# A fused attention and mixture-of-experts kernel: a newly searched order of the attention, a later place for the first weight loads, and nested conditional blocks at the end

## Chip, cores and metric

The kernel runs on one core of one Trainium2 chip. The metric is the device time of one execution in microseconds (us), from the first to the last instruction of the program with what lies around it. Before the change three executions took 914.98, 911.16 and 907.74 us; the median is 911.16 us.

## What is computed

Two layers follow one another. The first is causal attention with a decay, for 8 batches of 8 heads, 576 tokens and 64 numbers a head. The second sends each of the 4608 tokens to one of 8 experts, a two-layer network of its own.

```python
# attention, q k v: (8, 8, 576, 64), f: (8, 8, 576)
scores = q @ k.transpose(0, 1, 3, 2) / sqrt(64)
cum = cumsum(log(clip(f, 0.0001, 1.0)), axis=-1)
scores = where(causal, -1e9, scores + cum[..., :, None] - cum[..., None, :])
attn = exp(scores - max(scores)); attn = attn / (sum(attn) + 1e-9)
x = (attn @ v), heads side by side: (4608, 512)
# experts, w1: (8, 512, 1024), w2: (8, 1024, 512)
logits = x @ w_gate + modality_bias[modality_id]
e_idx = argmax(logits); gate_w = softmax(logits)[e_idx]
out[mask_e] = gate_w * (relu(x[mask_e] @ w1[e]) @ w2[e])
```

Products are split into high and low parts, so that each product of two tensors is three matmuls: high by high, high by low, low by high.

## The kernel before

**Attention, 32 pairs of heads.** Class `Attn` handles two heads (a pair, `p`) at a time. The work of a pair is cut into named steps, each a call of a small function on one engine: `hi` and `lo` split the loaded q and k (lines 347 and 353); `mm` (L486 to L497) are score matmuls for the row maxima, `mr` (L507 to L512) the maxima on VectorE; `sp` (L518) transposes them on TensorE, `ssp` (L524, L525) splits them, and `so` (L532, `shift_out`) stores them with two small DMAs into the tile `Sq`; `s` (L551 to L566) are the score matmuls that use `Sq`; `e` is the exponential, `h` and `r` split its result into `Ph` and `Pl` (L596, L604), `w` (L624 to L626) are the matmuls with v, and `d` (L635 to L640) divides by the row sum. Steps per batch prepare v (`v`, `vm`, `v1`, `v3`, `v2`, `vh`, `vl`), the gate (`vt`, `kg` at L437, `kh`, `kl`), and route and scatter the tokens (`ga`, `rt`, `sc`).

Matmuls of `mm` and `s` use 64 rows of TensorE's array, two heads beside one another; those of `w`, `kg`, `sp`, `rt` use 128 or fewer rows as one block. The profile writes the first as 64*128 and the second as 128*128.

**Who sets the order.** `Plan.order()` is a list scheduler. It holds every step's engine, a duration, its predecessors and the buffers it takes, and emits the steps one after another: among the ready ones the one whose earliest start is first, and where that is equal the one with the smaller due time, from the table `DUE`. The order it gives is the order of the program on each engine, since the attention runs under a manual schedule. The step `early`, put in when batch 5 has been scattered, makes the first table of the experts' tiles (25 small VectorE instructions, L915 to L986) and loads the first two tiles of tokens.

**Experts.** Class `Moe` takes the tokens, sorted by expert, in tiles of 256 (`FULL` = 21 of them at most) and then half tiles of 128 (8 at most). A tile `t` transposes its tokens (`prepare`), multiplies by w1 (`first`, L1083, 96 matmuls), by w2 (`second`, L1094, 48 matmuls) and scatters its rows with an indirect DMA on GpSimd (L1097). Meanwhile it loads the next weights on SyncE's queue (`load_w1` L1037, `load_w2` L1043) and splits them on ScalarE and VectorE (`split_w1` L1049 and L1050, `split_w2` L1056 and L1057). The loads of the first w1 (2 MB in two DMAs) are issued as soon as their space is free, in the place that the tile scheduler finds, which is inside the attention's last pairs.

How many tiles there are is known only on the chip. Tiles 0 to 13 always run. Tiles 14 to 20, and the 8 half tiles, each stand in a conditional block of their own, one after another; in this data 18 tiles and 3 half tiles run, so 3 blocks and then 5 blocks are skipped:

```python
            if t < ALWAYS:
                body()
            else:
                with self.tc.If(nt > t - EARLY):   # L1176
                    body()
        for t in range(8):
            with self.tc.If(nh > t):               # L1179
                self.half(t)
```

A skipped block still has to raise the semaphores that its instructions would have raised. On each engine that is a COMPARE_BRANCH and an EVENT_SEMAPHORE, and on GpSimd, for the DMAs that it would have issued, an INC_SWDGE_SEM. L1262 is the end of the program.

Of the kernel before, what the change touches and what calls it, by code (L numbers as in the profile page):

```python
# [26 lines left out]
P = 128  # L27
# [33 lines left out]
def f32(ap):  # L61
# [21 lines left out]
}  # L83


class Plan:


    LAT = {"PE": 0.15, "ACT": 0.15, "DVE": 0.1, "POOL": 0.18, "SP": 0.0}

    def __init__(self, rings):
        self.bufs = dict(rings)
        self.steps = {}

# [6 lines left out]
    def order(self):  # L101
# [8 lines left out]
        done, ef, dma = {}, dict.fromkeys(self.LAT, 0.0), 0.0  # L110
# [4 lines left out]
        while ready:  # L115
            best = None
            for n in ready:
                s = st[n]
                t = max((done[a] for a in s["after"]), default=0.0)
                blocked = False  # L120
                for j, (r, _) in enumerate(s["take"]):
                    k = len(taken[r]) - self.bufs[r] + j
                    if k >= 0:
                        x = given.get((r, taken[r][k]))
                        blocked = blocked or x is None
                        t = max(t, x or 0.0)
# [14 lines left out]
            for e, d in s["ops"]:  # L141
                port, e = e[3:] == "*", e.rstrip("*")
# [5 lines left out]
            if s["lands"] is not None:  # L148
                dma = max(dma, t) + s["lands"] / 190e3
# [21 lines left out]
class Attn:  # L171
# [355 lines left out]
    def shift_out(self, p):  # L527
# [3 lines left out]
        for a in range(2):  # L531
            self.nc.sync.dma_start(self.Sq[32 * a:P:64, p % 3, :], mT[:, a])  # L532
# [202 lines left out]
    def steps(self, early):  # L735
# [4 lines left out]
        def add(name, key, eng, t, fn, args, after=(), due=0.0, **kw):  # L740
# [8 lines left out]
            plan.add((name,) + key, ops, lambda: fn(*args), after, PER * at + DUE[kind], **kw)  # L749
# [4 lines left out]
        for p in range(n):  # L754
# [6 lines left out]
            add("hi", k, "ACT", 1.25, self.split_hi, k, [("raw", p) if p > 1 else None] + [prev("s", 3, g) for g in range(4)], d - 3)  # L761
            add("lo", k, "POOL" if p else "DVE", 2.8, self.split_lo, k, [("hi", p)], d + 2)
            add("cum", k, "SP", 0.55, self.put_cum, k, [prev("s", 3, g) for g in range(4)], d - 4, lands=10e3)
            for g in range(3):
                add("mm", k + (g,), "PE", (0.68, 0.68, 0.65)[g], self.max_mms, (p, g), [("hi", p), ("cum", p)], d + g,
                    take=[("ps", ("m", p, i)) for i in ((0,), (1,), (2, 3))[g]])
            for g in range(4):
                add("mr", k + (g,), "DVE", (1.4, 1.4, 0.77, 0.77)[g], self.max_red, (p, g),
                    [("mm", p, min(g, 2)), ("mr", p, 2) if g == 3 else None, prev("sp", 2)], d + g + 1, free=[("ps", ("m", p, g))])
            add("sp", k, "PE", 0.2, self.shift_pe, k, [("mr", p, g) for g in range(4)], d + 6, take=("pb", ("t", p)))  # L770
            add("ssp", k, "DVE", 0.6, self.shift_split, k, [("sp", p), prev("so", 2)], d + 6.3, free=[("pb", ("t", p))])
            add("so", k, "SP", 1.1, self.shift_out, k, [("ssp", p)] + [prev("s", 3, g) for g in range(4)], d + 7, lands=10e3)
            for g in range(4):
                add("s", k + (g,), "PE", (0.65, 0.55, 1.22, 1.17)[g], self.scores, (p, g), [("so", p), ("lo", p), ("cum", p)], d + 11 + g,
                    take=("ps", (p, g)))
                add("e", k + (g,), [("ACT", (0.74, 0.74, 1.08, 1.12)[g])], 0, self.exp, (p, g),
                    [("s", p, g)] + ([("e", p, 0)] if g == 1 else []), d + 12 + g,
                    free=[] if g == 2 else [("ps", (p, g))], take=None if g in (1, 2) else ("Pt", (p, max(g - 1, 0))))
            for i in range(3):
                gs = ((0, 1), (2,), (3,))[i]  # L780
                add("h", k + (i,), "ACT", (1.17, 1.02, 1.05)[i], self.half, (p, i),
                    [("e", p, g) for g in gs] + ([("w", 2 * p - 4), ("w", 2 * p - 3)] if p > 1 else [("setup2",)]), d + 13.5 + i)
                add("r", k + (i,), "DVE" if i == 1 else "POOL", (2.4, 1.21, 2.33)[i], self.rest, (p, i), [("h", p, i)], d + 15 + i,
                    free=[("ps", (p, 2)) if i == 1 else ("Pt", (p, i))])
            for h in range(2):
                u = 2 * p + h
                add("w", (u,), "PE", 1.55, self.weighted, (u,), [("r", p, i) for i in range(3)] + [("vl", b, c) for c in range(NJ)] + [("kl", b, p % 4)],
                    d + 19 + h, take=("po", u))
                add("d", (u,), "DVE", 1.12, self.divide, (u,),
                    [("w", u), ("gb", b)] + ([("sc", b - 2, c) for c in range(NJ)] if b > 1 else []), d + 20.5 + h, free=[("po", u)])  # L790
        for b in range(nb):
# [7 lines left out]
            for i in range(3):  # L799
                add("vm", k + (i,), "DVE", (1.2, 1.2, 0.7)[i], self.v_max, (b, i),  # L800
# [7 lines left out]
            for i in range(3):  # L808
                add("vh", k + (i,), "ACT", (1.15, 1.15, 0.72)[i], self.v_hi, (b, i),
                    [("v2", b), ("setup2",)] + ([("w", NH * (b - 1) - 1)] if b > 1 else []), d - 9 + i)  # L810
            for c in range(NJ):
                add("vl", k + (c,), "DVE*", 0.75, self.v_lo, (b, c), [("vh", b, c // 2)] + ([("w", NH * (b - 1) - 1)] if b > 1 else []), d - 7 + c)
            add("gb", k, "ACT", 0.3, self.gate_bias, k, [("gs",), ("setup2",), bp("ga", 2)], d - 5)
            add("gv", k, "ACT", 0.25, self.gate_part, k, [("gs",), ("v2", b), bp("kg", 2, 3)], d - 11)
            for hp in range(4):
# [4 lines left out]
                add("kg", k + (hp,), "PE", 1.22, self.key_gate, (b, hp), [("vt", b, hp), ("gv", b), ("kg",) + divmod(4 * b + hp - 1, 4) if b or hp else None] + free, d - 6 + hp, take=("pb", ("kg", b, hp)))  # L820
                add("kh", k + (hp,), "ACT", 0.3, self.key_gate_hi, (b, hp), [("kg", b, hp), ("setup2",)], d - 5.5 + hp)
                add("kl", k + (hp,), "DVE", 0.3, self.key_gate_lo, (b, hp), [("kh", b, hp)], d - 5 + hp, free=[("pb", ("kg", b, hp))])
# [10 lines left out]
            for c in range(NJ):  # L833

                add("sc", k + (c,), "POOL", 1.25, self.scatter, (b, c), [("sc", b, c - 1) if c and b < nb - 1 else ("rt", b, 6)], e + 8 + c, lands=263e3)
# [30 lines left out]
class Moe:  # L866
    def __init__(self, keep, tc, w1, w2, xs, writers, out):
# [18 lines left out]
        self.xgh, self.xhh, self.xlh = {}, {}, {}  # L886

    def open(self, ctx):
        ec, tc = ctx.enter_context, self.tc
        w = "tile"  # L890
        px = [ec(tc.tile_pool(name="c_px", bufs=1, space=PSUM, reuse_waits=w))]
        self.ps_h = ec(tc.tile_pool(name="c_ph", bufs=3, space=PSUM, reuse_waits=w))
        self.ps_y = ec(tc.tile_pool(name="c_py", bufs=2, space=PSUM, reuse_waits=w))
        px.append(ec(tc.tile_pool(name="c_px1", bufs=1, space=PSUM, reuse_waits=w)))
        self.px = lambda i: px[i].tile([P, 512], F32, name=f"px{i}")
# [8 lines left out]
        self.hx = ec(tc.tile_pool(name="c_hx", bufs=3, reuse_waits=w))  # L904
# [119 lines left out]
    def load_x(self, t):  # L1024
        nc = self.nc
        r = self.val(self.row[t], 1, 8 * (CAP // T) - 1)
        xg = self.keep.tile([P, 2, 514], F32, name="xg", bufs=3)
# [4 lines left out]
    def load_w1(self, row, i=0):  # L1032
# [3 lines left out]
        for q in range(2):  # L1036
            nc.sync.dma_start(self.raw1[i][:, :, q * 512:q * 512 + 512], w1[:, :, q * 512:q * 512 + 512], cond=self.ec[1])  # L1037
# [21 lines left out]
    def prepare(self, t):  # L1059
# [3 lines left out]
        xh = self.xp.tile([P, 4, T], F32R, name="xh", bufs=2)  # L1063
        xl = self.xp.tile([P, 4, T], F32R, name="xl", bufs=2)
# [23 lines left out]
    def second(self, xg, n):  # L1088
        nc = self.nc
        for c in range(n):  # L1090
            py = self.ps_y.tile([P, 512], F32, name="py")
# [3 lines left out]
            y = self.wk.tile([P, 512], F32, name="y", bufs=2)  # L1095
# [5 lines left out]
    def load_xh(self, t):  # L1101
        nc = self.nc
        r = self.val(self.rowh[t], 1, 8 * (CAP // T) - 1)
        xg = self.hx.tile([P, 514], F32, name="hxg", bufs=3)
# [3 lines left out]
    def prepare_h(self, t):  # L1108
        nc = self.nc
        xh = self.wk.tile([P, 4, P], F32R, name="hxh", bufs=2)  # L1110
        xl = self.wk.tile([P, 4, P], F32R, name="hxl", bufs=2)
# [7 lines left out]
    def first_h(self, t):  # L1119
# [3 lines left out]
        hb = self.wk.tile([P, 2, 512], F32, name="hb", bufs=1)  # L1123
        for q in range(2):
            ph = self.ps_h.tile([P, 2, T], F32, name="ph").rearrange("p a n -> p (a n)")
# [18 lines left out]
    def run(self, acc):  # L1144
        self.load_w1(self.row[0])
# [3 lines left out]
        self.prepare(0)  # L1149
        for t in range(FULL):  # L1150
# [22 lines left out]
            if t < ALWAYS:  # L1173
                body()
            else:
                with self.tc.If(nt > t - EARLY):  # L1176
                    body()
        for t in range(8):
            with self.tc.If(nh > t):  # L1179
# [19 lines left out]
def fused(tc, qk, v, vt, f, ids, wg, bias, w1, w2, out):  # L1199
    nc = tc.nc  # L1200
    with ExitStack() as top:
# [16 lines left out]
        with ExitStack() as ctx:  # L1218
            moe.open(ctx)
            moe.run(acc)  # L1220
# [45 lines left out]
```

## Time and profile before

| what | value |
|---|---|
| median of three executions | 911.16 us |
| the profiled execution's own time | 912.28 us |
| its span, first to last instruction | 910.3 us |
| mean granted TensorE clock | 0.966 |
| TensorE busy, share of the span | 826.5 us, 91% |
| VectorE busy | 644.7 us, 71% |
| ScalarE busy | 522.5 us, 57% |
| GpSimd busy | 380.8 us, 42% |
| data moved by DMA | 108.54 MB |

The attention fills the first 414 us, the experts' full tiles the time to 837 us, the half tiles that to 893 us. PE is TensorE's matmuls, PEld its weight loads, DVE VectorE, ACT ScalarE, POOL GpSimd, SP SyncE; a letter q behind them (POOLq) means the instruction queue of that engine: semaphores, branches, DMA issues. PEclk is the granted clock as a share of the full one.

### The profile page before, as it was taken

To read this page: it belongs to the slowest core of one execution; us is meant where nothing else is said; L and a number is where in the kernel's file an instruction comes from. 1 tells how busy PE (TensorE), PEld (TensorE's weight loads), DVE (VectorE), ACT (ScalarE), POOL (GpSimd) and SP (SyncE) were. 2 spreads that over 40 slices of the span, in tenths; PEclk is the share of its full clock that TensorE was granted. 3 is DMA by queue.
4 is the path that set the end of the run, shared out by engine and by line. 5 is a ranking of instruction groups with operands and counts; after the bars stand their busy time and mean duration, and the time that the engine had idled before them with its cause. 6 is when DMAs were issued, how large, how long until landed. Compare 5 with 4: busy or idle time off the path is not lost. (4 is left out here: it accounts for less than half of the span.)

```text
span 910.3 us, 23626 instructions
## 1 busy us (share of the span) xinstructions
PE 826.5 (91%) x9702; PEld 737.8 (81%) x9702; DVE 644.7 (71%) x1215; ACT 522.5 (57%) x640; POOL 380.8 (42%) x345
## 2 busy tenths in 40 slices
PE   3899999999999999668999999999999999997791
PEld 2688887878787878557899999999999999996571
DVE  7678888888889898566956666666666656664581
ACT  3568878787878776465445444444444444442570
POOL 9356787878787877454531111111111101110010
PEclk9799999999999999789999999999999999999796
DMA  5333443435344532414177511111114320136530
GB/s 195 104 101 112 156 151 126 153 127 152 128 152 125 155 125 69 151 38 152 70 276 269 225 66 47 47 47 47 48 47 141 122 75 29 47 136 232 197 128 3
DMA packets 43303, 108.54 MB, mean 119 GB/s; under 512 B 5423, under 2 KB 5615, under 8 KB 43184
## 3 DMA queue, kind: packets, MB, share of 16 engines
q1 hardware_dynamic: 36480, 85.87, 28.6%
q0 software_dynamic: 6704, 21.02, 5.9%
q8 instruction: 82, 1.34, 0.6%
q14 instruction: 37, 0.30, 0.1%
HBM read 144.19 MB, written 21.80 MB: 182 GB/s over the span
## 5 line engine op out<-in xcount | busy, mean ns | idle before, releaser
L1097 POOL DMA_INDIRECT out_dram<-y,xg x36 | 48.5, 1346 | 348.5 <-DVE y L1096 329.0
L604 POOL TENSOR_TENSOR Pl<-Pt,Ph 128x1152 f16<-128x1152 f32 (+1 forms) x64 | 144.8, 2262 | 61.3 <-ACT Ph L596 47.8
L1083 PE MATMUL ph<-xh,w1h 128*128 128x256 f32 x576 | 162.8, 283 | 2.2 <-ACT xh L1071 1.8
L1083 PE MATMUL ph<-xl,w1h 128*128 128x256 f32 x576 | 163.1, 283 | 0.2 <-DVE xl L1072 0.2
L1083 PE MATMUL ph<-xh,w1l 128*128 128x256 f32 x576 | 162.8, 283 | 0.0
L1056 ACT CAST w2h<-raw 128x1024 fp32r<-128x1024 f32 x84 | 86.3, 1048 | 119.3 <-PE py L1094 73.5
L1057 DVE TENSOR_TENSOR w2l<-raw,w2h 128x1024 fp32r<-128x1024 f32 x84 | 100.2, 1220 | 58.9 <-ACT w2h L1056 57.5
L1050 DVE TENSOR_TENSOR w1l<-raw,w1h 128x1024 fp32r<-128x1024 f32 x80 | 99.2, 1251 | 57.6 <-ACT w1h L1049 57.5
L1049 ACT CAST w1h<-raw 128x1024 fp32r<-128x1024 f32 x80 | 82.9, 1047 | 84.7 <-PE ph L1083 48.3
L1094 PE MATMUL py<-w2h,hh 128*128 128x512 f32 x312 | 120.6, 395 | 0.0
L1094 PE MATMUL py<-w2h,hl 128*128 128x512 f32 x312 | 119.1, 390 | 0.0
L1094 PE MATMUL py<-w2l,hh 128*128 128x512 f32 x312 | 118.9, 389 | 0.0
L566 PE MATMUL ps<-X 64*128 64x288 f32 (+4 forms) x1152 | 113.5, 324 | 0.0
L624 PE MATMUL po<-vh,Ph 128*128 128x73 f16 x960 | 105.5, 199 | 8.5 <-DVE lgh L640 8.5
L1083 PEld LDWEIGHTS ph<-xh,w1h 128*128 128x128 f32 x576 | 110.1, 192 | 3.7 <-ACT xh L1071 2.4
L1083 PEld LDWEIGHTS ph<-xl,w1h 128*128 128x128 f32 x576 | 110.4, 192 | 1.3 <-DVE xl L1072 0.4
L1083 PEld LDWEIGHTS ph<-xh,w1l 128*128 128x128 f32 x576 | 110.4, 192 | 0.0
L624 PEld LDWEIGHTS <-Ph 128*128 128x128 f16 x960 | 94.3, 99 | 15.7 <-issue 10.7
L626 PE MATMUL po<-vh,Pl 128*128 128x73 f16 x960 | 105.0, 199 | 0.5
L625 PE MATMUL po<-vl,Ph 128*128 128x72 f16 x960 | 105.2, 197 | 0.0
L581 ACT ACTIVATE Pt<-ps,lnp 128x576 f32<-128x576 f32 (+1 forms) x96 | 81.7, 867 | 30.2 <-PE ps L566 30.2
L566 PEld LDWEIGHTS ps<-X 64*128 64x128 f32 x1152 | 92.6, 197 | 5.2 <-issue 0.4
(273 smaller groups left out, 1876.4 us busy)
## 6 DMA issues: line engine op xcount, KB each, us to landing
raw<-in_w_dram SPq DMA_DIRECT2D x84, 1024.0 KB
raw<-in_qk_dram SPq DMA_DIRECT2D x32, 608.0 KB
xg<-xs SPq DMA_DIRECT2D x20, 514.0 KB
vT<-in_vt_dram SPq DMA_DIRECT2D x32, 320.0 KB
vr<-in_v_dram SPq DMA_DIRECT2D x30, 256.0 KB
raw1b<-in_w_dram SPq DMA_DIRECT2D x4, 1024.0 KB
hxg<-xs SPq DMA_DIRECT2D x5, 257.0 KB
Sq<-mT SPq DMA_DIRECT2D x64, 2.5 KB
```

Source lines behind the costliest of these rows:

```text
L566: nc.tensor.matmul(ps[:, h, c0:c0 + w], X[r, x, k], X[r, y, q], start=False, stop=(j == 2), skip_group_check=True)
L581: nc.scalar.activation(self.get("Pt", (p, i))[:, :, o:o + w], ps[:, :, 0:w], AF.Exp, bias=self.lnp, scale=0.125)
L604: e.tensor_tensor(self.Pl_t[p % 2][:, :, c], self.exps(p, i), self.Ph_t[p % 2][:, :, c], ALU.subtract)
L624: nc.tensor.matmul(o, Ph[:, c0:c0 + P], vh[:, c, hh, :], start=(c == 0), stop=False)
L625: nc.tensor.matmul(o[:, 1:73], Ph[:, c0:c0 + P], vl[:, c, hh, :], start=False, stop=False)
L626: nc.tensor.matmul(o, Pl[:, c0:c0 + P], vh[:, c, hh, :], start=False, stop=(c == ic))
L1049: nc.scalar.copy(self.w1h[a], self.raw1[i][a])
L1050: nc.vector.tensor_tensor(self.w1l[a], self.raw1[i][a], f32(self.w1h[a]), ALU.subtract)
L1056: nc.scalar.copy(self.w2h[a], self.raw2[a])
L1057: nc.vector.tensor_tensor(self.w2l[a], self.raw2[a], f32(self.w2h[a]), ALU.subtract)
L1083: nc.tensor.matmul(ph[:, i, :], w[:, k, f0:f0 + P], x[:, k, :], start=(j == 0), stop=(j == len(m) - 1))
L1094: nc.tensor.matmul(py, h[:, k, c * P:c * P + P], w[:, k, :], start=(j == 0), stop=(j == len(m) - 1))
```

## The change

Four things change.

1. `Plan` has a new model of the machine: a matmul step that uses 64 rows is marked `^`, and a change between the two kinds of steps costs `TURN`; most durations are shorter, and the latencies behind a step differ by engine. The table `DUE` is new, and steps of the first two and the last two pairs have due times of their own (`'a'`, `'z'`). No step's instructions change; their order does.
2. `load_w1` for tile 0 takes the name of the attention's last shift DMA, and the scheduler may put the two loads only behind it.
3. The conditional blocks of tiles 14 to 20 are nested: block 15 stands inside block 14, and so on. The same holds for the 8 half tiles. The first false condition leaves the whole nest.
4. Tiles that were taken from pools with several buffers (`xg`, `xh`, `xl`, `ph`, `py`, `y`, `hxh` and others) are now allocated once and used in turn, with the same numbers of buffers as before.

```diff
 DUE = {
-    ('setup2',): 111.41, ('gs',): 878.08, ('hi',): -66.01, ('lo',): -36.62, ('cum',): -40.34, ('mm', 0): 49.44,
...
+    ('setup2',): 59.93, ('gs',): -20.52, ('hi',): -36.28, ('lo',): 13.75, ('cum',): 310.53, ('mm', 0): 56.83,
...
+    ('v', 0): -36.04, ('v', 1): 13.45, ('early',): -47.68, ('hi', 'a'): 38.30, ('hi', 'z'): -41.08,
...
+EACH = ("raw", "hi", "lo", "cum", "mm", "mr", "sp", "ssp", "so", "s", "e", "h", "r", "w", "d")
 class Plan:
-    LAT = {"PE": 0.15, "ACT": 0.15, "DVE": 0.1, "POOL": 0.18, "SP": 0.0}
+    TURN = 0.092
+    RATE = 280e3
+    LAT = {"PE": 0.22, "ACT": 0.145, "DVE": 0.12, "POOL": 0.13, "SP": 0.0}
...
-                key = (max(t, ef[e] + 0.12), s["due"])
+                key = (max(t, ef[e] + 0.12) + (self.TURN if e == "PE" and half != rows else 0.0), s["due"])
...
+                if e == "PE" and half != rows:
+                    d, rows = d + self.TURN, half
...
-                dma = max(dma, t) + s["lands"] / 190e3
+                dma = max(dma, t) + s["lands"] / self.RATE
...
         for a in range(2):
-            self.nc.sync.dma_start(self.Sq[32 * a:P:64, p % 3, :], mT[:, a])
+            x = self.nc.sync.dma_start(self.Sq[32 * a:P:64, p % 3, :], mT[:, a])
+        self.shifted = x.ins.name
...
-            plan.add((name,) + key, ops, lambda: fn(*args), after, PER * at + DUE[kind], **kw)
+            end = "a" if name in EACH and at < 2 else "z" if name in EACH and at >= n - 2 else ""
+            plan.add((name,) + key, ops, lambda: fn(*args), after, PER * at + DUE[kind + (end,) if end else kind], **kw)
...
-                add("mm", k + (g,), "PE", (0.68, 0.68, 0.65)[g], self.max_mms, (p, g), [("hi", p), ("cum", p)], d + g,
+                add("mm", k + (g,), "PE^", (0.66, 0.66, 0.62)[g], self.max_mms, (p, g), [("hi", p), ("cum", p)], d + g,
...
-    def load_w1(self, row, i=0):
+    def load_w1(self, row, i=0, behind=None):
...
-            nc.sync.dma_start(self.raw1[i][:, :, q * 512:q * 512 + 512], w1[:, :, q * 512:q * 512 + 512], cond=self.ec[1])
+            x = nc.sync.dma_start(self.raw1[i][:, :, q * 512:q * 512 + 512], w1[:, :, q * 512:q * 512 + 512], cond=self.ec[1])
+            if behind:
+                why = mybir.DependencyInfo(mybir.DependencyClass.NoSync, mybir.DependencyReason.SCHED_ONLY)
+                self.tc.add_manual_dep(x.ins, behind, why, reason="large loads would hold up the last shifts")
...
-            if t < ALWAYS:
-                body()
-            else:
-                with self.tc.If(nt > t - EARLY):
-                    body()
-        for t in range(8):
-            with self.tc.If(nh > t):
+            if t >= ALWAYS:
+                nest.enter_context(self.tc.If(nt > t - EARLY))
+            body()
+        nest.close()
+        with ExitStack() as nest:
+            for t in range(8):
+                nest.enter_context(self.tc.If(nh > t))
                 self.half(t)
...
-            moe.run(acc)
+            moe.run(acc, a.shifted)
```

More of the change, by code (lines that the diff above doesn't have):

```diff
@@ L93, in __init__, with kind @@
         self.steps = {}
+    @staticmethod
+    def kind(e):
+        return e.rstrip("*^"), e.endswith("*"), e.endswith("^")
     def add(self, name, ops, fn, after=(), due=0.0, take=None, free=(), lands=None):
@@ L760, in steps @@
                 add("raw", k, "SP", 0.4, self.load_raw, k, [prev("lo", 2), prev("hi", 2)], d - 8, lands=622e3)
-            add("hi", k, "ACT", 1.25, self.split_hi, k, [("raw", p) if p > 1 else None] + [prev("s", 3, g) for g in range(4)], d - 3)
-            add("lo", k, "POOL" if p else "DVE", 2.8, self.split_lo, k, [("hi", p)], d + 2)
+            add("hi", k, "ACT", 1.11, self.split_hi, k, [("raw", p) if p > 1 else None] + [prev("s", 3, g) for g in range(4)], d - 3)
+            add("lo", k, "POOL" if p else "DVE", 2.74, self.split_lo, k, [("hi", p)], d + 2)
@@ L780, in steps @@
                 gs = ((0, 1), (2,), (3,))[i]
-                add("h", k + (i,), "ACT", (1.17, 1.02, 1.05)[i], self.half, (p, i),
+                add("h", k + (i,), "ACT", (1.06, 0.9, 0.95)[i], self.half, (p, i),
                     [("e", p, g) for g in gs] + ([("w", 2 * p - 4), ("w", 2 * p - 3)] if p > 1 else [("setup2",)]), d + 13.5 + i)
-                add("r", k + (i,), "DVE" if i == 1 else "POOL", (2.4, 1.21, 2.33)[i], self.rest, (p, i), [("h", p, i)], d + 15 + i,
+                add("r", k + (i,), "DVE" if i == 1 else "POOL", (2.35, 1.14, 2.15)[i], self.rest, (p, i), [("h", p, i)], d + 15 + i,
                     free=[("ps", (p, 2)) if i == 1 else ("Pt", (p, i))])
@@ L833, in steps @@
             for c in range(NJ):
-                add("sc", k + (c,), "POOL", 1.25, self.scatter, (b, c), [("sc", b, c - 1) if c and b < nb - 1 else ("rt", b, 6)], e + 8 + c, lands=263e3)
+                add("sc", k + (c,), "POOL", 1.12, self.scatter, (b, c), [("sc", b, c - 1) if c and b < nb - 1 else ("rt", b, 6)], e + 8 + c, lands=263e3)
         if early:
@@ L886, in __init__, with ring, next @@
         self.xgh, self.xhh, self.xlh = {}, {}, {}
+        self.rings, self.used = {}, {}
+        self.ring("xg", keep, 3, [P, 2, 514], F32)
+    def ring(self, name, pool, n, shape, dt):
+        self.rings[name] = [pool.tile(shape, dt, name=f"{name}{i}", bufs=1) for i in range(n)]
+        self.used[name] = 0
+    def next(self, name):
+        r, i = self.rings[name], self.used[name]
+        self.used[name] = i + 1
+        return r[i % len(r)]
     def open(self, ctx):
@@ L890, in open, with psum @@
         w = "tile"
[L891 to L895, printed above, removed]
+        def psum(name, n):
+            pool = ec(tc.tile_pool(name="c_" + name, bufs=1, space=PSUM, reuse_waits=w))
+            self.ring(name, pool, n, [P, 512], F32)
+        psum("px0", 1)
+        psum("ph", 3)
+        psum("py", 2)
+        psum("px1", 1)
+        self.px = lambda i: self.next(f"px{i}")
         def one(shape, dt, name):
@@ L1026, in load_x @@
         r = self.val(self.row[t], 1, 8 * (CAP // T) - 1)
-        xg = self.keep.tile([P, 2, 514], F32, name="xg", bufs=3)
+        xg = self.next("xg")
         self.xg[t] = xg
@@ L1062, in prepare @@
         xg = self.xg[t]
-        xh = self.xp.tile([P, 4, T], F32R, name="xh", bufs=2)
-        xl = self.xp.tile([P, 4, T], F32R, name="xl", bufs=2)
+        xh = self.next("xh")
+        xl = self.next("xl")
         self.xh[t], self.xl[t] = xh, xl
@@ L1077, in first @@
         for g in range(4):
-            ph = self.ps_h.tile([P, 2, T], F32, name="ph")
+            ph = self.next("ph").rearrange("p (a n) -> p a n", a=2)
             for i in range(2):
@@ L1090, in second @@
         for c in range(n):
-            py = self.ps_y.tile([P, 512], F32, name="py")
+            py = self.next("py")
             m = [(k, h, w) for k in range(8) for h, w in ((self.hh, self.w2h), (self.hh, self.w2l), (self.hl, self.w2h))]
@@ L1094, in second @@
                 nc.tensor.matmul(py, h[:, k, c * P:c * P + P], w[:, k, :], start=(j == 0), stop=(j == len(m) - 1))
-            y = self.wk.tile([P, 512], F32, name="y", bufs=2)
+            y = self.next("y")
             nc.vector.tensor_scalar(y, py, xg[:, c, 512:513], None, ALU.mult)
@@ L1103, in load_xh @@
         r = self.val(self.rowh[t], 1, 8 * (CAP // T) - 1)
-        xg = self.hx.tile([P, 514], F32, name="hxg", bufs=3)
+        xg = self.next("hxg")
         self.writers.before(nc.sync.dma_start(xg, self.xs.rearrange("(n p) e -> p n e", p=T)[0:P, bass.ds(r, 1), :]))
@@ L1109, in prepare_h @@
         nc = self.nc
-        xh = self.wk.tile([P, 4, P], F32R, name="hxh", bufs=2)
-        xl = self.wk.tile([P, 4, P], F32R, name="hxl", bufs=2)
+        xh = self.next("hxh")
+        xl = self.next("hxl")
         self.xhh[t], self.xlh[t] = xh, xl
@@ L1122, in first_h @@
         xh, xl = self.xhh[t], self.xlh[t]
-        hb = self.wk.tile([P, 2, 512], F32, name="hb", bufs=1)
+        hb = self.next("hb")
         for q in range(2):
-            ph = self.ps_h.tile([P, 2, T], F32, name="ph").rearrange("p a n -> p (a n)")
+            ph = self.next("ph")
             m = [(k, x, w) for k in range(4) for x, w in ((xh, self.w1h), (xh, self.w1l), (xl, self.w1h))]
@@ L1142, in early, with run @@
             self.load_x(t)
-    def run(self, acc):
-        self.load_w1(self.row[0])
+    def run(self, acc, behind):
+        self.load_w1(self.row[0], 0, behind)
         self.load_w2()
@@ L1149, in run @@
         self.prepare(0)
+        nest = ExitStack()
         for t in range(FULL):
```

40 lines of the change are left out of this document (22 added, 18 removed), and 40 rows, old and new, of the table DUE.

## The prediction, made before the changed kernel was run

> **What bounds the kernel now.** I read the span cut into its stages first. The columns are the stage, its length, the busy time of each engine (with its instructions), the granted clock, the DMA share and GB/s.
>
> ```profile
> core 0: us, PE busy (x) PEld busy (x) DVE busy (x) ACT busy (x) POOL busy (x), PEclk, DMA share, GB/s
> 12.00:36.00 24.00, 16.55 (x210) 12.71 (x209) 20.46 (x41) 10.80 (x14) 14.59 (x19) 0.94 0.41 136
> 36.00:80.00 44.00, 43.86 (x697) 38.49 (x696) 32.24 (x72) 30.72 (x37) 24.53 (x11) 0.84 0.35 117
> 80.00:360.00 280.00, 267.71 (x5227) 237.47 (x5227) 245.39 (x597) 214.62 (x262) 230.22 (x182) 1.00 0.43 136
> 360.00:414.00 54.00, 35.94 (x653) 31.29 (x649) 33.90 (x97) 26.41 (x30) 25.72 (x27) 0.84 0.25 88
> 432.00:837.00 405.00, 405.00 (x2619) 370.28 (x2617) 257.33 (x330) 192.12 (x239) 59.40 (x44) 1.00 0.31 108
> 837.00:848.00 11.00, 0.16 (x2) 0.06 (x1) 0.75 (x1) 0.70 (x1) 0.98 (x1) 0.73 0.33 119
> 848.00:893.00 45.00, 40.41 (x180) 31.89 (x180) 35.53 (x36) 30.37 (x39) 4.39 (x3) 0.95 0.44 159
> 893.00:910.30 17.30, 0.00 (x0) 0.00 (x0) 0.00 (x0) 0.00 (x0) 0.00 (x0) 0.50 0.01 2
> ```
>
> The full tiles (432 to 837) are TensorE's without a gap; nothing in the change shortens their matmuls. The attention's body (80 to 360) is TensorE's to 96%, with VectorE at 88% and GpSimd at 82% close behind. Four places hold idle time: the attention's start and its last 54 us, the 11 us at 837, and the 17.3 us after the last busy instruction. The change touches all four.
>
> **The skipped blocks at 837.** The waits and the instruction queues name the cause.
>
> ```profile
> PE ph L1128 <- PEq L1176: 10.8, 1, 10.8
> ACT w2h L1056 <- PEq L1176: 19.5, 1, 19.5
> L1176 PEldq COMPARE_BRANCH  x4: 169/3428/6702, 832.9 to 843.5; - x4
> L1176 PEldq EVENT_SEMAPHORE  x3: 51/51/51, 839.9 to 847.2; - x3
> 836.74 0.39 PE L1094 MATMUL py<-w2h,hl 128*128 128x512 f32 x1
> 847.97 0.77 PE L1128 MATMUL ph<-w1h,hxh 128*128 128x512 f32 x1 [10.84 <-PEq L1176]
> ```
>
> TensorE's queue goes through three skipped blocks one by one, up to 6.7 us for a branch; its three semaphore raises stand at 839.9 to 847.2. ScalarE's first cast of the half tiles waits for the last of them. Nested, the first false condition leaves all three: one branch and one raise. The first (to 839.9) stays, two go: 847.2 − 839.9 = **7.3 us**. Nothing else is late then: the half tile's tokens and weights were loaded before (SyncE issues nothing that it waits for here), and GpSimd is next needed at 864. Bounds: if closing the nest costs two branches like the others on the way out, the gain is 7.3 − 2 × 3.4 = 0.5; if the shorter pause also keeps the clock up, it is more. For that see how the clock fell:
>
> ```profile
> 838.00:840.00 2.00, 0.00 (x0) 0.00 (x0) 0.00 (x0) 0.00 (x0) 0.00 (x0) 1.00 0.82 309
> 840.00:844.00 4.00, 0.00 (x0) 0.00 (x0) 0.00 (x0) 0.00 (x0) 0.98 (x1) 0.74 0.06 20
> 844.00:848.00 4.00, 0.03 (x1) 0.06 (x1) 0.00 (x0) 0.70 (x1) 0.00 (x0) 0.50 0.18 59
> 848.00:852.00 4.00, 4.00 (x10) 3.13 (x11) 3.62 (x4) 3.19 (x4) 0.00 (x0) 0.50 0.04 7
> ```
>
> It fell near 842 (0.74 over 4 us), 5 us after the last matmul, and then ran 4 us at half. The new pause would be 837.1 to 840.7, 3.6 us. By the row it stays warm, and up to 4 × 0.5 = 2 us more are won; I count 0 of it, as after 374 (below) the clock fell after some 3.3 us. The Trainium skill (TensorE: Matmul & The Clock Gate, HAM oscillation) says that an idle window of about 3.4 us sends the clock to half; by that rule the sum stays as I have it, and by the row alone it is 2 us lower.
>
> **The skipped blocks at the end.**
>
> ```profile
> 891.92 0.98 POOL L1097 DMA_INDIRECT out_dram<-y,hxg  x1 [11.85 <-DVEq L1179]
> L1179 POOLq INC_SWDGE_SEM  x5: 1875/1880/1892, 892.0 to 900.4; - x5
> L1179 PEldq EVENT_SEMAPHORE  x5: 51/51/51, 890.8 to 895.0; - x5
> L1262 POOLq DRAIN  x1: 7182/7182/7182, 902.3 to 902.3; - x1
> L1262 POOLq EVENT_SEMAPHORE  x4: 17/17/17, 909.5 to 910.2; - x4
> ```
>
> GpSimd decides: five INC_SWDGE_SEM, one for each skipped half tile, (900.4 − 892.0) / 4 = 2.1 us apart, then a drain of 7.2 us, then the end. Nested there is one, and four go: 4 × 2.1 = **8.4 us**. TensorE's skip ends at 895.0, before the drain would. Bounds: 0, if the drain waits for something that ends at 909.5 anyway; 8.4 + 7.2 × 4/5 = 14.1, if it also handles what the five raised. I take 8.4, since a wait that starts behind the fifth raise moves with it.
>
> **The last shifts.** The order of the SyncE queue, and who waits:
>
> ```profile
> 370.85 1.21 SPq L1037 DMA_DIRECT2D raw<-in_w_dram  x2
> L532 SPq DMA_DIRECT2D Sq<-mT x4: 495/518/588, 372.3 to 383.7; - x4
> PE ps L558 <- DMA Sq<-mT: 4.0, 1, 4.0
> 374.50:378.50 4.00, 0.00 (x0) 0.00 (x0) 2.63 (x9) 0.00 (x0) 3.37 (x3) 0.91 0.87 335
> 378.50:386.00 7.50, 7.48 (x100) 6.23 (x102) 1.32 (x7) 2.57 (x3) 2.28 (x7) 0.60 0.01 3
> 396.26 3.88 ACT L1049 CAST w1h<-raw 128x1024 fp32r<-128x1024 f32 x4
> ```
>
> The 2 MB of w1 are issued 1.4 us before a shift of 2.5 KB a DMA; the engines move 335 GB/s while TensorE waits 4.0 us for that shift, and the matmuls after it run at 0.60 of the clock. With the loads behind the last shift these **4.0 us** go. The clock's part (7.5 × 0.4 = 3.0) I leave out: other pauses are near. The move passes the two last pairs' four shift DMAs on SyncE. The two w1 DMAs then issue at 383.7 + 0.5 + 1.2 = 385.4 and take 2.1 MB / 335 GB/s = 6.3, so land near 392, or 394 with a slow start; their first reader is the cast at 396.26. That cover is 2 to 4 us; if it is gone, each us of lateness is one before the first full tile. Bounds: 0 (late weights give it back) to 7.
>
> **The order.** Three kinds of loss stand in the rows. First, row-mode changes:
>
> ```profile
> 360.77 0.20 PE L625 MATMUL po<-vl,Ph 128*128 128x72 f16 x1
> 360.80 0.20 PE L626 MATMUL po<-vh,Pl 128*128 128x73 f16 x1
> 360.93 0.30 PE L492 MATMUL ps<-Sk,Cq 64*128 64x288 bf16 x2
> 81.71 0.27 PE L518 MATMUL pb<-ident,mt 128*10 128x128 f32 x1
> 358.85 0.53 PE L497 MATMUL ps<-X 64*128 64x192 f32 x4
> L518 PE MATMUL pb<-ident,mt 128*10 128x128 f32 x25 | 6.9, 275 | 0.0
> ```
>
> Starts follow one another by 0.03, and by 0.13 where the kind changes: 0.1 lost. From 80 to 360 I count 160 changes (the first behind 81.71, the last behind 358.85) for 25 pairs (the L518 row), 6.4 a pair. A pair needs at least two; at five a pair 1.4 × 25 × 0.1 = 3.5 us go. Second, TensorE's 280 − 267.7 = 12.3 idle us there, in waits of 0.6 and less. VectorE's 245.4 busy leaves room to 88%, so a third of them is a fair share: 4. I take 5 for both together. Third, the ends:
>
> ```profile
> PE ps L558 <- DVE mt L507: 3.4, 1, 3.4
> PE po L624 <- DVE lgh L640: 8.5, 4, 6.3
> 397.34 3.84 DVE L1050 TENSOR_TENSOR w1l<-raw,w1h 128x1024 fp32r<-128x1024 f32 x3
> ```
>
> At 364 TensorE waited 3.4 us for maxima that stood behind `early`'s small instructions on VectorE; before the last `w` it waited 6.3 us for a division that stood behind the first splits of w1. Both can move: `early` has a new due time, the last two pairs their own, and the splits shift with the loads. I take 3 of these 9.7 and 2 of the start's idle time (24 − 16.55 = 7.4). So the order is worth 5 + 3 + 2 = **10 us**. Bounds: +10 (a plan that fits its model and not the machine) and −25 (all 12.3 idle, 6 more of changes and 7 at the ends).
>
> **At nothing:** the tiles allocated once. Buffers keep their numbers, so each reuse waits for the same reader; the full tiles' TensorE at 405.00 of 405.00 covers it, and without that cover a pause of 0.6 us as at `mr` in each of 18 tiles would cost 11.
>
> **The sum.** 7.3 + 8.4 + 4.0 + 10 = 29.7 us. The profiled execution took 912.28, 1.1 above the median of 911.16: 912.28 − 29.7 = 882.6, or 881.5 against the median. I say 882.
>
> **The rivals.**
> - *The order gives nothing.* For it: TensorE is 96% busy in the body, and a gap closed on one engine may open on VectorE at 88%. Against: 6.4 mode changes a pair and two waits above 3 us are plain. 912.3 − 19.7 = 892.
> - *The order reaches far.* The start's cold clock (0.84 over 36 to 80, 7 us) and most idle time go: 25 instead of 10, 867. Against: VectorE's 245.4 in 280.
> - *The drain does not move.* The tail keeps its 909.5: 882.6 + 8.4 = 891. For it: nothing in the rows says what it waits for.
> - *The nest is not left in one go.* Each level has its own branch and raise, so neither skip gets shorter and the change doesn't do what it says: 882.6 + 15.7 = 898.
> - *Slower: VectorE becomes the bound.* In-order VectorE, 88% busy, gets divisions ahead of maxima, as `early` stood at 364; TensorE then waits in each of 32 pairs. The other gains are 19.7, so from 0.6 us a pair it decides; at 1 us a pair the kernel takes 912.3 − 19.7 + 32 = 925.
>
> **How the numbers follow.** The forecast 0.55; the order gives nothing 0.16; far 0.14; the drain 0.06; the nest 0.05; slower 0.04. A measurement of this kernel tells about 1% from no change, 9 us. Under 902 lie all but the last, half of the nest's cases and a few of a weak order: faster 0.91, same 0.05, slower 0.04. The range takes in the far order (867) and the nest as it is (898).
>
> **What would show it.** The semaphore raises of L1176 on TensorE's queue fall to one, and TensorE's pause there to under 5 us; one INC_SWDGE_SEM at L1179, and the span ends 18 to 19 us after the last `y` scatter's start falls to about 10. L1037's first issue follows L532's last, and TensorE's wait for `Sq` is under 1 us. Mode changes fall to about five a pair, and the first full tile starts 14 us earlier. It is wrong if the time to the first full tile hardly moves, if the drain grows by what the raises lost, or if the first cast of w1 waits for its load.

## The result and the profile after

The changed kernel takes **881.27 us** (median of four executions, 877.34 to 882.74) against 910.19 us for the kernel before in the same session (four, 907.74 to 914.98): a ratio of 0.967, with a 95% interval of 0.962 to 0.972. The forecast was 882. The profiled execution took 882.74 us, its span is 881.0 and its mean granted clock 0.981.

The stages of the kernel after, in the columns used above (length, busy time of each engine, granted clock, DMA share, GB/s):

```profile
36.00:80.00 44.00, 42.34 (x804) 37.69 (x802) 37.50 (x83) 35.64 (x43) 29.38 (x13) 0.96 0.38 119
80.00:340.00 260.00, 249.12 (x4966) 223.76 (x4968) 239.51 (x569) 203.71 (x249) 213.17 (x175) 1.00 0.44 143
340.00:399.00 59.00, 44.58 (x834) 39.76 (x830) 40.19 (x117) 32.39 (x38) 34.02 (x36) 0.90 0.27 91
399.00:822.00 423.00, 422.10 (x2745) 386.92 (x2744) 269.99 (x352) 203.82 (x254) 64.27 (x61) 0.99 0.31 110
822.00:826.50 4.50, 0.28 (x2) 0.00 (x0) 0.75 (x1) 0.81 (x1) 0.00 (x0) 1.00 0.75 274
826.50:871.40 44.90, 40.07 (x180) 31.66 (x180) 35.54 (x36) 30.26 (x39) 9.17 (x4) 0.96 0.48 165
871.40:881.00 9.60, 0.00 (x0) 0.00 (x0) 0.00 (x0) 0.00 (x0) 0.00 (x0) 0.50 0.01 1
```

Between five landmarks of the two timelines (first matmul of the full tiles, last one, first matmul of the half tiles, start of the last `y` scatter, end of the span) the time went like this:

| stage | before | after | saved | predicted |
|---|---|---|---|---|
| start to first full tile | 414.2 | 399.7 | 14.5 | 14.0 (order 10, shifts 4) |
| full tiles | 422.9 | 422.6 | 0.4 | 0 |
| pause before the half tiles | 10.8 | 4.4 | 6.4 | 7.3 |
| half tiles | 43.95 | 43.74 | 0.2 | 0 |
| last scatter to the end | 18.4 | 10.6 | 7.8 | 8.4 |
| span | 910.3 | 881.0 | 29.3 | 29.7 |

**The nests.** Instruction queues of the kernel after, then the timelines of TensorE and GpSimd at the two nests, then two stretches behind the first:

```profile
L1226 PEldq COMPARE_BRANCH  x6: 65/78/7430, 725.9 to 825.8; - x6
L1226 PEldq EVENT_SEMAPHORE  x1: 51/51/51, 825.6 to 825.6; - x1
L1227 POOLq INC_SWDGE_SEM  x1: 1892/1892/1892, 870.9 to 870.9; - x1
L1312 POOLq DRAIN  x3: 51/107/7182, 873.0 to 880.7; - x3
```

```profile
821.89 0.39 PE L1143 MATMUL py<-w2h,hl 128*128 128x512 f32 x1
826.68 0.47 PE L1177 MATMUL ph<-w1h,hxh 128*128 128x512 f32 x1 [4.40 <-issue]
870.42 0.98 POOL L1146 DMA_INDIRECT out_dram<-y,hxg  x1 [8.51 <-DVEq L1227]
```

```profile
826.00:828.00 2.00, 1.32 (x4) 1.11 (x5) 1.24 (x2) 2.00 (x3) 0.51 (x1) 0.77 0.06 18
828.00:830.00 2.00, 2.00 (x6) 1.54 (x6) 2.00 (x2) 1.58 (x2) 0.85 (x1) 0.50 0.30 111
```

One semaphore raise instead of three on TensorE's queue, and one long branch (7.43 us, the longest of six). At the end there is one INC_SWDGE_SEM instead of five. The drain's longest is 7182 ns, as before. The clock still falls behind the pause, to 0.50.

**The last shifts.** SyncE's queue, then TensorE's wait:

```profile
362.47 7.76 SPq L556 DMA_DIRECT2D Sq<-mT  x4
371.78 1.11 SPq L1083 DMA_DIRECT2D raw<-in_w_dram  x2
```

```profile
PE ps L583 <- DMA Sq<-mT: 0.8, 1, 0.8
PE po L649 <- DVE lgh L665: 9.1, 5, 4.4
```

The loads now issue behind the last shift, and the wait for `Sq` fell from 4.0 to 0.8. The longest wait of a late `w` for a division is 4.4 where it was 6.3.

**Mode changes.** Counted on TensorE's timeline from 80 to 340 (matmuls of 64*128 next to 128*128), 106 in 23 pairs, 4.6 a pair; the kernel before has 151 in the same stretch. First and last change, and the row that counts the pairs:

```profile
81.65 0.39 PE L521 MATMUL ps<-X 64*128 64x288 f32 x2
339.58 0.26 PE L576 MATMUL ps<-later,id 64*128 64x128 bf16 x4
L542 PE MATMUL pb<-ident,mt 128*10 128x128 f32 x23 | 6.3, 275 | 0.0
```

**What the sum hides.** "Full tiles, 0" came out at 0.4, but of two parts that cancel. Stretches at 0 and at 12 us of the full tiles, in the kernel before and then in the kernel after:

```profile
414.20:418.20 4.00, 3.85 (x30) 3.64 (x31) 2.04 (x10) 1.79 (x3) 1.81 (x6) 1.00 1.03 372
426.20:438.20 12.00, 10.28 (x60) 8.64 (x59) 11.05 (x33) 2.02 (x3) 6.80 (x4) 1.00 0.30 99
```

```profile
399.70:403.70 4.00, 3.98 (x18) 3.97 (x19) 2.02 (x9) 2.17 (x3) 0.46 (x2) 0.50 0.88 336
411.70:423.70 12.00, 11.77 (x64) 9.83 (x63) 11.06 (x11) 4.60 (x6) 5.39 (x4) 1.00 0.29 106
```

The kernel after begins its full tiles at half clock, 18 matmuls in 4 us instead of 30. It has 0.23 us without a matmul 12 us later, where the kernel before has 1.72.

### The profile page after: what moved, and what is told of

Its sections match the earlier page's. It is cut to its first block, busy times and chain, and to the rows that moved or that the text cites. A ratio compares the mean times of both kernels' runs of the same rounds, so it can differ in the third digit from the quotient of the medians.

```text
span 881.0 us, 23519 instructions
## 1 busy us (share of the span) xinstructions
PE 819.0 (93%) x9702; PEld 735.8 (84%) x9702; DVE 649.2 (74%) x1215; ACT 521.1 (59%) x640; POOL 371.0 (42%) x345
## 3 DMA queue, kind: packets, MB, share of 16 engines
q1 hardware_dynamic: 36480, 85.87, 29.3%
## 5 line engine op out<-in xcount | busy, mean ns | idle before, releaser
L1146 POOL DMA_INDIRECT out_dram<-y,xg x36 | 45.6, 1266 | 352.0 <-DVE y L1145 336.7
L649 PE MATMUL po<-vh,Ph 128*128 128x73 f16 x960 | 105.9, 200 | 12.7 <-DVE lgh L665 10.9
L377 POOL TENSOR_TENSOR X<-raw,X 128x1216 fp32r<-128x1216 f32 x31 | 85.9, 2770 | 63.3 <-ACT X L371 60.2
L649 PEld LDWEIGHTS <-Ph 128*128 128x128 f16 x960 | 95.0, 99 | 17.4 <-DVE lgh L665 10.6
L591 PE MATMUL ps<-X 64*128 64x288 f32 (+4 forms) x1152 | 107.1, 316 | 0.0
L606 ACT ACTIVATE Pt<-ps,lnp 128x576 f32<-128x576 f32 (+1 forms) x96 | 79.6, 865 | 43.6 <-PE ps L591 43.5
```

Source lines behind the costliest of these rows:

```text
L377: e.tensor_tensor(X[:, 1], self.get("raw", p), f32(X[:, 0]), ALU.subtract)
L591: nc.tensor.matmul(ps[:, h, c0:c0 + w], X[r, x, k], X[r, y, q], start=False, stop=(j == 2), skip_group_check=True)
L649: nc.tensor.matmul(o, Ph[:, c0:c0 + P], vh[:, c, hh, :], start=(c == 0), stop=False)
```

## The experiments

My theory: the four places are independent and add up; each mode change costs TensorE 0.1 us; a nest costs one branch and one raise. Rivals: the order alone does nothing, and the shifts' move carries what was put down to it; the drain or the branch grows back; late w1 returns the shifts' gain. Times are medians, differences in us against the median of the kernel before on the same chip. That kernel took 915.7, 909.1 and 915.8 us on the three chips of the experiments, so kernels of one chip are compared first.

### Each part alone

`order_only`: the kernel before with the new `Plan`, `DUE`, durations and marks.

> The kernel before with the new plan and due times alone; the first weight loads and the conditional blocks as before. Theory (the four terms add): about 10 us less than before, and a pause for the last shifts of up to 4 us stays, because the w1 loads may again stand ahead of them. Rival A (the order carries the whole 14.5 us by which the first full tile came earlier, and the place of the loads is worth nothing): 14 us less. Rival B (the order pays only with the loads moved): under 4 us less. The pause of 10.8 us between full and half tiles and the 18.4 us behind the last scatter's start stay in all cases.

`behind_only`: the kernel before with the loads of w1 behind the last shift.

```diff
-            moe.run(acc)
+            moe.run(acc, a.shifted)
```

> The kernel before with the first two w1 loads held behind the last shift and nothing else. Theory: 4 us less, TensorE's wait of 4.0 us for Sq gone. Rival (the late weights give it back): within 1 us of before, with ScalarE's first w1 cast waiting for its load, or the weight splits pushed later and the first full tile with them.

`nest_only`: the attention and `Plan` of before, the new `Moe` (nests and fixed tiles), loads of w1 where they were.

> The kernel before with nested conditional blocks and the tiles allocated once; old order, loads not held. Theory: 14 us less (6.4 between full and half tiles, 7.8 at the end, as the changed kernel's trace has them), attention and full tiles unchanged. Rival (the tiles allocated once change waits in the full tiles): the full tiles' 423 us differ by more than 1 us.

`after_not_behind`: the changed kernel without the move of the loads.

```diff
-            moe.run(acc, a.shifted)
+            moe.run(acc, None)
```

> The changed kernel with the w1 loads free again; the order on the other engines is the same, only SyncE's queue has the two 1 MB loads ahead of the last two pairs' four shifts. Theory: slower than the changed kernel by 2 to 4 us, with TensorE waiting that long for Sq once and a dip of the clock behind it. Rival (in the new order the shift has slack): within 1 us, and since the w1 casts no longer wait for their load (1.8 us) even faster.

| kernel | median | ratio to before, interval | saved | first full tile at |
|---|---|---|---|---|
| order_only | 904.89 | 0.987 (0.984 to 0.990) | 10.8 | 408.0 |
| behind_only | 912.73 | 0.995 (0.994 to 0.997) | 2.9 | 410.7 |
| nest_only | 900.48 | 0.982 (0.979 to 0.985) | 15.2 | 414.9 |
| after_not_behind | 886.37 | 0.968 (0.964 to 0.972) | 29.3 | 406.3 |

By the ratio the four savings would be 12.0, 4.3, 16.6 and 29.4. By the medians order and nest make 10.8 + 15.2 = 26.0, and `after_not_behind`, which is these two, saves 29.3: the parts add to within some 3 us. Most of these 3 is the pause and the half tiles behind it, which take 3.1 + 43.8 us in `nest_only` and 2.0 + 42.1 in `after_not_behind`; the first nest is not independent of what the clock does behind it. With the shifts' 2.9 the three make 28.9, and the changed kernel saves 35.9 on another chip where the kernel before takes the same 915.8 (`after_again`, below), so that the sum of the parts falls 7 short of the whole there. "The order gives nothing" falls.

Only the loads' place differs between the next two. SyncE's queue and TensorE's wait in `behind_only`, then in `after_not_behind`:

```profile
372.67 8.27 SPq L532 DMA_DIRECT2D Sq<-mT  x4
382.76 0.83 SPq L1038 DMA_DIRECT2D raw<-in_w_dram  x2
PE po L625 <- DVE lgh L641: 8.2, 3, 6.3
```

```profile
360.56 1.09 SPq L1083 DMA_DIRECT2D raw<-in_w_dram  x2
363.00 13.21 SPq L556 DMA_DIRECT2D Sq<-mT  x4
PE ps L583 <- DMA Sq<-mT: 4.7, 1, 4.7
```

With the loads ahead, the new order waits 4.7 us for its shift (5.6 in `order_only`) and the first full tile starts at 406.3, against 399.7 and 401.9 in two traces of the changed kernel. In the old order the move alone leaves the 6.3 us wait for the division, just as predicted for a step that belongs to the order.

Where the old order is run on this chip (`behind_only`, `nest_only`), the full tiles take 426.6 to 427.1, not the 422.9 of the first trace; on a third chip (`before_four_halves`) they take 426.7. `nest_only` at 0 and 12 us of them:

```profile
414.90:418.90 4.00, 3.85 (x18) 3.64 (x19) 2.02 (x10) 1.73 (x3) 1.78 (x6) 0.60 1.02 367
426.90:438.90 12.00, 9.50 (x56) 8.49 (x56) 10.22 (x23) 2.62 (x4) 5.92 (x4) 0.86 0.31 100
```

There the first tile starts cold (0.60) and then pauses 2.5 us. The new order starts it cold too and pauses 0.2. So on this chip some 4 us of the order's 10.8 fall inside the first full tile, and 414.9 − 408.0 = 6.9 before it. Why the first trace of the kernel before starts that tile at full clock was not found.

### What a mode change costs

One small matmul more in each pair's `mm`, into PSUM columns that nobody reads; in `turn128` it uses 128 rows, so that the kind changes, in its twin `turn64` it uses 64.

```diff
+        if g == 2:
+            nc.tensor.matmul(pm[:, 0, 320:384], self.Cq[0:P], self.Cq[0:P, 0:64], start=True, stop=True, ...)
```

> The changed kernel with one more small matmul in each of the 32 pairs, put between 64-row matmuls of a mm step into columns of PSUM that nobody reads; it uses 128 rows of the array, so it adds two row-mode changes a pair. Theory (a change costs 0.1 us of TensorE on the path): 32 x (2 x 0.1 + 0.03) = 7.4 us more than the changed kernel, less what falls into TensorE's 4% idle time; against its twin with 64 rows 6.4 us more. Rival (the changes hide in the pauses, the order's gain is shorter waits): under 2 us against the twin.

> The twin: the same small matmul at the same place with 64 rows, so no added row-mode change. Both theories: within 1.5 us of the changed kernel (32 x 0.03 = 1 us of TensorE).

The added matmul itself costs the same in both, in the groups of instructions:

```profile
L514 PE MATMUL ps<-Cq 128*128 128x64 bf16 x32 | 6.5, 204 | 1.6 <-DVE Pl L631 1.6
```

```profile
L514 PE MATMUL ps<-Cq 64*128 64x64 bf16 x32 | 6.4, 201 | 1.6 <-DVE Pl L631 1.6
```

`turn128` took 883.25 us (ratio 0.972, 0.969 to 0.974), `turn64` 880.51 (0.968, 0.965 to 0.971). The intervals touch, so the difference of 2.7 us is not sure by the times alone; the first full tile stands 2.5 us later (403.0 against 400.5), which agrees. My expectation counted the changes wrongly: in 15 of the 32 pairs the matmul ahead was already not one of 64 rows, and only 34 more changes stand in the timeline (182 against 148). At 0.1 each that is 3.4; 2.5 to 2.7 is 0.07 to 0.08 a change. So about three quarters of what the changes cost reach the first full tile and, as far as the medians tell, the end.

### The cover of w1

In the changed kernel the casts of w1 stand before the last `Ph` of the attention. ScalarE's timeline:

```profile
378.76 2.00 ACT L1098 CAST w1h<-raw 128x1024 fp32r<-128x1024 f32 x2
382.61 1.05 ACT L1098 CAST w1h<-raw 128x1024 fp32r<-128x1024 f32 x1 [1.84 <-DMA raw<-in_w_dram]
383.56 1.00 ACT L621 CAST Ph<-ps 128x1024 f16<-128x1024 f32 x1
384.46 1.05 ACT L1098 CAST w1h<-raw 128x1024 fp32r<-128x1024 f32 x1
385.41 1.15 ACT L621 CAST Ph<-Pt 128x1152 f16<-128x1152 f32 x1
```

`split_late` puts the casts behind the last `h` and the differences `w1l` behind the last `r`; `split_late2` holds part q of `w1l` behind the divisions of the last three `w`.

```diff
-            nc.scalar.copy(self.w1h[a], self.raw1[i][a])
-            nc.vector.tensor_tensor(self.w1l[a], self.raw1[i][a], f32(self.w1h[a]), ALU.subtract)
+            x = nc.scalar.copy(self.w1h[a], self.raw1[i][a])
+            y = nc.vector.tensor_tensor(self.w1l[a], self.raw1[i][a], f32(self.w1h[a]), ALU.subtract)
+            self.tc.add_manual_dep(x.ins, behind[0], why, ...)
+            self.tc.add_manual_dep(y.ins, behind[1], why, ...)   # split_late2: behind[1][q]
```

> The changed kernel with the first split of w1 held, in order only, behind the last pair's Ph casts on ScalarE and behind its Pl on VectorE. In the changed kernel the first w1 cast waits 1.8 us for its load at 382.6, with two Ph casts of the last pair queued behind it, and TensorE then idles for the last w. Theory (those casts set the end of the attention): the Ph casts come 4.7 and 5.5 us earlier and the first full tile starts 4 to 5 us earlier, the kernel is 4 to 5 us faster. Rival (the first full tile waits for its w1 splits, or another wait of the last pair takes over): under 1 us.

> As the run before it (the changed kernel with the w1 casts on ScalarE behind the last Ph), and on VectorE the four parts of the w1 split held behind the divisions of the last three w steps (one behind the 62nd, one behind the 63rd, two behind the last). Theory (what took over was the division, queued behind w1 splits while TensorE waited 5.7 us): the first full tile starts 3 to 4 us before the 398.0 of the run before, the kernel is 5 us faster than the changed one. Rival (the last w steps wait for their Pl from GpSimd, ready at 383.6, and the tile for its w1 splits): 1 us or less.

`split_late` took 877.87 us (0.965, 0.962 to 0.968). Its timelines of ScalarE and VectorE and its wait:

```profile
379.06 1.03 ACT L621 CAST Ph<-ps 128x1024 f16<-128x1024 f32 x1
379.95 1.19 ACT L621 CAST Ph<-Pt 128x1152 f16<-128x1152 f32 x1
...
382.12 2.56 DVE L1103 TENSOR_TENSOR w1l<-raw,w1h 128x1024 fp32r<-128x1024 f32 x1 [0.78 <-ACT w1h L1102]
```

```profile
PE po L652 <- DVE lgh L668: 9.3, 4, 5.7
```

The last `Ph` comes 385.41 − 379.95 = 5.5 us sooner, and yet the first full tile only 1.7 (398.0): the division (four small instructions on VectorE) now stands behind and between splits, the first of them 2.56 us long. With that mended too, `split_late2` starts its full tiles at 395.9 and takes 876.20 us (0.958, 0.955 to 0.961), 3.7 less than the changed kernel on its chip, where 5 were expected (`after_again`, whose interval overlaps; its first full tile is at 401.9). The wait for the division is down to 1.5, and a new wait of 3.2, for the tokens' split before the first full tile, is the longest there:

```profile
PE po L652 <- DVE lgh L668: 4.7, 4, 1.5
PE ph L1140 <- ACT xh L1128: 3.2, 1, 3.2
```

### The branch and the load beside it

In the changed kernel 2 MB of w1 for the second half tile are issued while TensorE goes through the branch (274 GB/s in the row of 822 to 826.5). `half_late` holds that load until the first matmul of the half tiles; `both2` is this and `split_late2`; `after_again` is the changed kernel once more.

```diff
-        if t < 7:
+        if 0 < t < 7:
             self.load_w1(self.rowh[t + 1], (t + 1) % 2)
...
             self.first_h(t)
+            if t == 0:
+                self.load_w1(self.rowh[1], 1, None, self.h0)
```

> The changed kernel with the 2 MB load of the second half tile's w1 held until TensorE has begun the first half tile. Theory (TensorE's branch out of the nest, 7.4 us here, fetches its target while those 2 MB are moved at 360 GB/s and is slowed by them; the skips that met no load took 3.3 to 3.6 us): the branch takes 3 to 4 us, the pause of 4.4 us falls under 1 us, the kernel is 3 to 4 us faster; the load still lands before ScalarE needs it 9 us after the first half tile's start. Rival (the branch takes its time for itself, waiting for TensorE's queue to empty): the branch stays at 7 us, and nothing is won, or the late load costs up to 3 us.

> The changed kernel once more, on the same chip as the next three, so that they can be compared: about 0.967 of before. Its pause between full and half tiles tells how far it differs between chips (4.4 us in the first trace, 2.0 to 3.1 in kernels with the same nest).

> The run before plus the held load of the second half tile's w1. If both gains are real and independent: 5 + 3 = 8 us faster than the changed kernel, first full tile near 395 and the pause between full and half tiles near 1 us. Rival: the gains overlap or trade against the clock, under 5 us.

The branch of TensorE's queue in `after_again`, `half_late` and `both2`:

```profile
L1226 PEldq COMPARE_BRANCH  x6: 65/78/4730, 728.2 to 825.3; - x6
```

```profile
L1231 PEldq COMPARE_BRANCH  x6: 65/78/3510, 726.4 to 822.9; - x6
```

```profile
L1239 PEldq COMPARE_BRANCH  x6: 65/78/3870, 723.1 to 819.7; - x6
```

Without the load the branch takes 3.5 and 3.9 us; in the seven other kernels with the nests whose load is issued meanwhile it takes 4.7 to 7.4. The branch out of the second nest, which meets no such load, takes 3.3 to 3.9 in all ten traces with the nests. The kernel before shows the same: of its three long branches the one beside a load took 6.7, the others 3.3 and 3.6. The pause falls to 1.1 us in both kernels (it then ends with VectorE's queue), but from 1.6 to 3.1 in the others of their chips, so little is left to win, and the 3 to 4 us of the expectation are not there: `half_late` took 877.33 us (0.964, 0.961 to 0.967), `both2` 875.01 (0.955, 0.953 to 0.957), and `split_late2` beside it 876.20, with intervals that overlap. That a taken branch whose target lies outside the code at hand has to wait for that code to be fetched is what the Trainium skill says (Runtime: NRT & Kernel Launch, Instruction fetch mechanics); that loads lengthen it is what these rows show, on two traces without the load and eight with it; what the loads and the branch share was not measured.

`after_again` took 879.88 us (0.960, 0.958 to 0.962). **`both2` is the best kernel: 4.9 us below the changed one on the same chip**, with intervals of the ratio that do not meet. The expected 8 are missed: the 3 of the held load are not there, as said.

### Is it the block or the nest

`before_four_halves`: the kernel before, one block after another as it was, with room for four half tiles, so that one block is skipped and not five. The three half tiles of this data are computed as before.

```diff
-        for t in range(8):
+        for t in range(4):
```

> The kernel before, all blocks one after another, but with room for 4 half tiles in place of 8 (this data needs 3, so the result is whole): one block is skipped at the end in place of five. Theory (each skipped block costs GpSimd 2.1 us, and the drain behind them is fixed): the tail falls by 4 x 2.1 = 8.4 us or the 7.8 us that nesting gave, the drain stays at 7.2 us, and nothing else moves. Rival (the nest saves by its form, a skipped block is not the unit of cost): the tail falls by less than 5 us.

```profile
896.95 0.98 POOL L1097 DMA_INDIRECT out_dram<-y,hxg  x1 [11.86 <-DVEq L1179]
L1179 POOLq INC_SWDGE_SEM  x1: 1880/1880/1880, 897.0 to 897.0; - x1
L1262 POOLq DRAIN  x3: 51/107/7182, 899.0 to 906.7; - x3
```

908.46 us (0.991, 0.988 to 0.993), 7.4 less than the kernel before. The tail is 907.0 − 896.95 = 10.05 us, as short as the nest's 10.58. What costs is a skipped block, (18.4 − 10.05) / 4 = 2.1 us each; that it stands in a nest is no saving of its own, and the drain is the same 7182 ns behind one raise as behind five.

## Why the prediction was right, and where it was not

**The first nest, 7.3: right in its mechanism.** One branch and one raise stay. The session of the result gives 6.4. Where the old and the new form were traced on one chip, it is 10.8 − 3.1 = 7.7 (`behind_only`, `nest_only`) and 10.2 − 1.6 = 8.6 (`before_four_halves`, `after_again`); the branch that stays sets the size, with 7.43, 6.19 and 4.73 us. The stated bound of 0.5, by two more branches on the way out, falls: one raise.

**The clock there, counted at 0: right in the first trace, wrong as a rule.** Behind the pause of 4.4 us the clock fell, and the half tiles took 43.7 us. Behind pauses of up to 2.4 us it stayed up, and they took 42.1 to 42.2, so the gain that "the row alone" put at 2 is 1.6; `after_again`, with a pause of 1.6, has it. Near 3.1 us both came out: 3.11 in `split_late` kept the clock, 3.09 in `nest_only` did not. For each, the first matmul behind the pause, and a stretch that shows the clock behind it:

```profile
823.74 0.47 PE L1184 MATMUL ph<-w1h,hxh 128*128 128x512 f32 x1 [3.11 <-PEq L1233]
824.00:826.00 2.00, 2.00 (x10) 1.63 (x10) 2.00 (x2) 2.00 (x3) 0.07 (x1) 1.00 0.26 95
```

```profile
844.60 0.47 PE L1151 MATMUL ph<-w1h,hxh 128*128 128x512 f32 x1 [3.09 <-PEq L1200]
844.00:848.00 4.00, 3.40 (x10) 2.70 (x11) 3.25 (x3) 3.56 (x4) 1.16 (x1) 0.72 0.31 118
```

So at this length the pause alone does not decide. The fall comes late, too. If the clock goes from 1.00 to 0.50 in one step, 0.72 over 844 to 848 puts it near 845.8, and 0.77 over 826 to 828 puts that of the kernel after near 827.1. These are 4.2 and 4.8 us after the last matmul before the pause, and matmuls were running again by then. The rule that the prediction quotes from the Trainium skill (about 3.4 us) agrees with these pauses to a few tenths.

**The second nest, 8.4: right** (7.8; 8.3 in `before_four_halves`). The rival that the drain stays where it was falls, and so does the bound of 14.1.

**The last shifts, 4.0: the sum right, one step wrong.** The move alone gives 2.9 by the medians and 414.9 − 410.7 = 4.2 at the first full tile, and the wait fell from 4.0 to 0.8. The step that failed is "their first reader is the cast at 396.26. That cover is 2 to 4 us". The changed order moves that cast to 378.76, ahead of the last `Ph`; it had no cover, waited 1.84 us for its load, which is one of the prediction's own signs of being wrong, and the attention's own casts stood behind it. The loads moved as well, from the 385.4 of the prediction to 371.8, but less far than the cast, and they took until 382.6, 10.8 us and not 6.6 to 8.6. I had taken the reader's place from the old trace, although the change reorders just that stretch. The lost cover did not eat the 4.0: without the move the first full tile comes 406.3 − 401.9 = 4.4 to 406.3 − 399.7 = 6.6 us later. It left unwon what `split_late2` shows, 6.0 us at the first full tile and 3.7 in the medians.

**The order, 10: right in size, and its parts only roughly.** Alone it gives 10.8 on a chip where 4 of them are in the first full tile. The mode changes fell by 45 from 80 to 340, at 0.1 us 4.5; the prediction had 3.5 for them, and `turn128` shows that about three quarters of such a price reach the end. In idle time the body has 260 − 249.12 = 10.9 us, where the kernel before has 12.2 in this stretch, so a gain of 1.3:

```profile
80.00:340.00 260.00, 247.78 (x4847) 219.28 (x4846) 229.00 (x561) 199.41 (x243) 213.29 (x170) 1.00 0.44 140
```

The start is worth more than its 2: counted by matmuls done, the kernel after is some 78 ahead at 80 us, about 4 us, as the clock from 36 to 80 is 0.96 and not 0.84 (0.96 to 1.00 in all ten traces of the new order, 0.82 to 0.84 in the four of the old). At 340 it is some 197 ahead, about 10 us. The ends give the other 4 (14.5 at the first full tile), with the shifts' 4 in them. So most of the order's gain came early, from the clock and the mode changes, and the ends hardly moved, for the reason above. In `order_only`, with the loads ahead of the shifts, the lead at the first full tile is only the 6.9. "VectorE becomes the bound" didn't come, though VectorE is now busy 239.51 of 260 (229.00 before): 92%.

**Fixed tiles, 0: right as a sum**, with the clock's loss and the shorter pause in it as shown; which of the changes shortens the pause is told by `order_only`, which has the old tiles and the short pause: the order.

**The sum, 29.7 forecast and 28.9 measured: close in part by luck.** On the chip of `after_again` the same change saves 35.9. `before_four_halves` has the old attention and the old first blocks on that chip; against it `after_again` gains 14.1 us up to the first full tile, 4.0 in the full tiles, 8.6 in the pause and 1.9 in the half tiles. In the first two traces the kernel before happened to start its full tiles at full clock, and the kernel after had the longest branch of all; both make the saving smaller. The mechanisms hold on both chips; that the total met the forecast within 1 us is not owed to them alone.

Open: why the kernel before differs by 5 to 6 us between chips, beyond the cold first tile; why the parts alone add to 7 us less than the whole on another chip, beyond the 3 at the pause; and what makes the branch 4.73 or 7.43 us in the same kernel.

## What to carry to other kernels

When a change reorders a stretch, the first reader of a moved load has to be looked for in the new order, since the cover in the old trace says nothing about it. Count what is paid per skipped block and per engine, and not only the branch: here GpSimd's raise, which no busy share shows, was with five times 1.9 us the longest item of the tail. Where a pause ends close to the point at which the clock falls, a load held back by a few us is worth trying, though here its own gain (1.2 us, `both2` against `split_late2`) is not clear of the noise.

## What the runs showed of the hardware

- A row-mode change between matmuls costs 0.07 to 0.1 us (0.1 between the starts of neighbours; 34 added: 2.5 to 2.7 us).
- A taken branch on TensorE's queue, over a full tile or out of a nest, took 3.3 to 3.9 us, and 4.7 to 7.4 beside 2 MB of loads; at the five skipped half tiles, one block after another, no branch took more than 2.9 (`behind_only`).
- GpSimd's drain at the program's end took 7182 ns whether one or five INC_SWDGE_SEM of 1.9 us stood before it.
- The clock stayed at 1.00 behind a pause of 3.11 us and fell behind one of 3.09; where it fell behind 3.09 and 4.40, it did so 4.2 and 4.8 us after the last matmul.
